# A fused cross-attention and maxout-FFN kernel: batch 0 loaded as fp32 by the hardware queue, batch 2 transposed by the array, token loads issued once per period

## The chip, the core and the metric

The kernel runs on one core of a Trainium2 chip. The core has a matrix array (TensorE, PE in the profile), three engines for element-wise work (VectorE or DVE, ScalarE or ACT, GpSimd or POOL) and a sequencer that issues DMAs and does no arithmetic (SyncE or SP). Each engine works through its own list of instructions in order, and engines wait for each other and for DMAs by semaphores. The array writes to a small memory of eight banks (PSUM), from which ACT or DVE copies results ("evicts" them) to the working memory. DMAs issued by SP and ACT go through a hardware queue, those issued by POOL through a software queue[...]. The metric is the device time of one execution, in microseconds.

## What is computed

There are 8 batches with 8 heads of 512 tokens and 32 state vectors, 64 wide. Tokens read the state, the state reads the tokens, and the 544 rows per batch go through a feed-forward layer with a maximum over three products:

```
scores  = x @ state.T / 8          # 512 x 32 per batch and head
xread   = softmax(scores)  @ state # 512 x 64
sread   = softmax(scores.T) @ x    # 32 x 64
r       = concat([xread, sread]), heads side by side   # 4352 x 512
h       = max(r @ w1, r @ w2, r @ w3)                  # 4352 x 768
out     = h @ w_out                                    # 4352 x 512, fp32
```

## The kernel before, in words

The state is first multiplied into the weights: for every batch b and every 128 columns m of the hidden layer, `m_unit` (M in the lists) forms M = state x W for all heads and three weight matrices. Each M unit is eight small matmuls into two banks, evicted by two copies of 384 columns on the engines that two letters name (aa: both on ACT, av: ACT and DVE). Then the hidden layer of the token rows is softmax x M. That is `up` (u): two matmuls into one bank for each of the three matrices i. For i = 0 ACT copies the bank (line 292), for i = 1 and 2 DVE takes the maximum with it (lines 296 and 298). `out_half` (o) multiplies the hidden rows with w_out, three matmuls for each half; after the second half a copy to fp32 and, after every two row tiles, a store of 512 KB on SP's queue (line 327).

The softmax of a batch needs these steps:

- `load_x` (lx, line 146): POOL issues a DMA that reads 1 MB of fp32 tokens and writes 512 KB of bf16. All batches lie side by side in one buffer, x_sb.
- `permute_x` (pm, line 207): a copy that brings the heads of a token together (tile xn), by the engine that the letter names (v DVE, g POOL, a ACT), for half of the token tiles or for all (a dash).
- the transposed tokens xT, in one of two ways: `x_array` (xT), eight transposing matmuls per half and a copy from the bank; or `x_crossbar` (xb, line 212), one transposing DMA on SP's queue.
- `scores` (S, two halves): 8 matmuls, exp on ACT (line 230), row sums and reciprocals on DVE (234, 237), and a multiply on POOL or DVE (238) into the tile a.
- the transposed softmax aT, by the array (`a_array`, aT) or by a transposing DMA (`a_crossbar`, ab or X, line 243).
- `state_reads` (R): the other direction, 24 matmuls, a reciprocal and two multiplies on DVE.

Nothing is ordered by a planner: every engine gets its instructions in the order in which the program emits them. That order is written by hand in three lists. OPENING (line 28) holds the first two batches' hidden layers and batch 0's output, token by token; `lw 0 1` loads W for columns of m = 0, `lo` loads w_out, `id`, `sel` and `idle` make the identity, transpose the state and run dummy matmuls. After it PERIOD runs six times and LAST once (loop from line 379). In a period, u belongs to the group g = 2, 3, 4, 5, 6 and then the state rows (group 8), o to the group before, S, X and R to the batch after (nb = t + 2), M to batches taken from a queue, and P permutes batch nb + 1 on POOL and transposes it by the crossbar. In LAST g is batch 7. The order of the letters is the order on the array; on POOL and SP the same order holds only among the few instructions that these engines get.

On POOL the order in the opening is: tokens 0, W (m = 0), tokens 1, W (4 and 5), permutations, W (1), W (2 and 3), tokens 2 and 3, two softmax multiplies, w_out, the permutation of batch 2, tokens 7, the permutation of batch 3, tokens 6 and 4, the multiplies of batch 2, tokens 5. From there on POOL only multiplies and permutes. SP issues the state load, the crossbar transposes of batches 2 and 3, and then for each period the transposes of a and of the next xn and two stores.

Of the kernel before, what the change touches and what calls it, by code (L numbers as in the profile page):

```python
# [8 lines left out]
F32 = mybir.dt.float32  # L9
BF16 = mybir.dt.bfloat16  # L10
# [15 lines left out]


OPENING = """
id, idle 9, sel, idle 9, lx 0, lw 0 1, lx 1, pm 0 0 v, lw 4 6, pm 0 1 g, lw 1 2,
xT 0 0 v, xT 0 1 v, pm 1 0 g, pm 1 1 g, S 0 0 v, M 2 0 aa, S 0 1 v, M 1 0 aa, idle 4,  # L30
lw 2 4, lx 2, M 0 0 aa, aT 0 0 v, R 0, xT 1 0 a, lx 3, aT 0 1 a, xT 1 1 v, S 1 0 g,
u 0 0 0, M 0 4 aa, M 0 5 av, u 0 0 1, u 0 0 2, S 1 1 g, lo, u 0 4 0, u 0 5 0, M 0 1 aa,
u 0 5 1, u 0 4 1, u 0 5 2, M 1 1 aa, u 0 4 2, M 1 4 aa, u 0 1 0, pm 2 - g, aT 1 - v,
xb 2, u 0 1 1, M 0 3 va, M 0 2 va, u 0 1 2, u 1 0 0, u 1 4 0, lx 7, pm 3 - g, u 1 1 0,
lx 6, u 1 0 1, u 0 3 0, u 1 4 1, u 0 2 0, M 1 2 aa, M 1 5 av, xb 3, u 1 4 2, u 0 2 1,
u 1 0 2, u 0 2 2, M 1 3 aa, M 2 3 aa, u 0 3 1, u 0 3 2, u 1 1 1, u 1 2 0, u 1 3 0,
u 1 5 0, u 1 1 2, u 1 5 1, lx 4, u 1 5 2, o 0 0 0 a, o 0 0 1 a, u 1 2 1, S 2 1 g,
S 2 0 g, ab 2, u 1 3 1, o 0 1 0 v, M 2 2 aa, R 1, o 0 1 1 a, o 0 2 0 v, M 2 4 aa,
u 1 2 2, o 0 2 1 a, o 0 3 0 a, M 2 5 aa, M 2 1 va, u 1 3 2, o 0 3 1 v, R 2, lx 5
"""  # L40


PERIOD = """
o o u u u u S S o o M M m u R u o u o X u u u u u u u P u u o u o u m M M
"""
LAST = """
M M u u u M u u S M u u u u u S u u u u P M R M u o u o u u o X o o o o o
"""


# [1 line left out]
def kernel(  # L52
# [14 lines left out]
    nc = tc.nc  # L67

    B, H, S, D = x.shape
# [5 lines left out]
    J = S // 128  # L75
# [6 lines left out]

    const = ctx.enter_context(tc.tile_pool(name="const", bufs=1))
    res = ctx.enter_context(tc.tile_pool(name="res", bufs=1))
    xnp = ctx.enter_context(tc.tile_pool(name="xnp", bufs=3))
    att2 = ctx.enter_context(tc.tile_pool(name="att2", bufs=2))
    tmpp = ctx.enter_context(tc.tile_pool(name="tmpp", bufs=4))
    htp = ctx.enter_context(tc.tile_pool(name="htp", bufs=2))
    op = ctx.enter_context(tc.tile_pool(name="op", bufs=2))
# [3 lines left out]
    def bank(shape, dt, name):  # L93
        return psum.tile(shape, dt, tag="bank", name=name)
# [3 lines left out]
    def copy(eng, o, i):  # L98
        if eng == "a":
            nc.scalar.copy(out=o, in_=i)  # L100
        else:
            ENG[eng].tensor_copy(out=o, in_=i)  # L102

    def mm(out_ap, lhsT, rhs, start, stop, pos=(0, 0)):
        nc.tensor.matmul(out_ap, lhsT, rhs, start=start, stop=stop, tile_position=pos)  # L105

    def tr(out_ap, in_ap):
# [8 lines left out]
    nc.sync.dma_start(  # L116
        out=st32.rearrange("p n d -> p (n d)"),
        in_=state.rearrange("b h (q n) d -> (b h q) (n d)", q=2))
    zeros = const.tile([128, 512], BF16, name="zeros")
    nc.vector.memset(zeros, 0.0)  # L120
    sbd = res.tile([128, B, HP, 2, Ns], BF16, name="sbd")
# [7 lines left out]

    W = res.tile([128, 3, HP, d_ff], BF16, name="W")  # L130
    wout = res.tile([128, MT, d_model], BF16, name="wout")
    x_sb = res.tile([128, B, H, J, D], BF16, name="x_sb")
    M_sb = res.tile([128, B, MT, 2, 3, 128], BF16, name="M_sb")
    AT = res.tile([128, HP, ST], BF16, name="AT")
    w_v = [w.rearrange("(kk p) f -> p kk f", p=128) for w in (moe_w1, moe_w2, moe_w3)]
# [6 lines left out]
    def load_wout():  # L142
        nc.gpsimd.dma_start(out=wout, in_=moe_w_out.rearrange("(kk p) f -> p kk f", p=128))

    def load_x(b):
        nc.gpsimd.dma_start(  # L146
            out=x_sb[:, b].rearrange("p h j d -> p h (j d)"),
            in_=x[b].rearrange("h (p j) d -> p h (j d)", j=J))


# [36 lines left out]
    def tile_of(kind, b, pool, shape):  # L187
        if (kind, b) not in tiles:
            tiles[kind, b] = pool.tile(shape, BF16, tag=kind, name=kind)
        return tiles[kind, b]  # L190

    def x_nat(b):
        return tile_of("xn", b, xnp, [128, J, H, D])

    def xT(b):
        return tile_of("xT", b, att2, [128, J, HP, 128])
# [9 lines left out]

    def permute_x(b, h, eng):
        j = slice(0, J) if h is None else slice(2 * h, 2 * h + 2)
        copy(eng, x_nat(b)[:, j], x_sb[:, b, :, j].rearrange("p h j d -> p j h d"))

    def x_crossbar(b):
        nc.sync.dma_start_transpose(
            out=xT(b).rearrange("p j hp t -> p (j hp) t"),
            in_=x_nat(b).rearrange("p j h d -> p (j h d)"))
# [27 lines left out]
    def a_crossbar(b):  # L242
        nc.sync.dma_start_transpose(
            out=aT(b).rearrange("p j a t -> p (j a) t"),
            in_=a_of(b).rearrange("p j a hp n -> p (j a hp n)"))
# [32 lines left out]
    def up(g, m, i):  # L278

        nn = S if g < B else ST  # L280
        ht = tile_of("ht", g, htp, [128, MT, S])
        pw = bank([128, S], F32, "pw")
        if g < B:
            for par in range(2):
                mm(pw, M_sb[:, g, m, par, i, :], aT(g)[:, :, par, :], par == 0, par == 1)
        else:
            for hp in range(HP):
                mm(pw[:, :nn], W[:, i, hp, m * 128:(m + 1) * 128], AT[:, hp, :],
                   hp == 0, hp == HP - 1)
        if i == 0:  # L290
            t = tiles["t", g, m] = tmpp.tile([128, S], BF16, tag="t0", name="t0")
            nc.scalar.copy(out=t[:, :nn], in_=pw[:, :nn])  # L292
        elif i == 1:
            t0 = tiles["t", g, m]
            t = tiles["t", g, m] = tmpp.tile([128, S], BF16, tag="t1", name="t1")
            nc.vector.tensor_max(t[:, :nn], t0[:, :nn], pw[:, :nn])  # L296
        else:
            nc.vector.tensor_max(ht[:, m, :nn], tiles["t", g, m][:, :nn], pw[:, :nn])  # L298

    def out_half(g, j, h, eng):  # L300
        last = g == ORDER[-1]
        if h == 0:
            tiles["po"] = bank([128, d_model], F32, "po")
        po = tiles["po"]
        for kt in range(3 * h, 3 * h + 3):
            mm(po, tiles["ht", g][:, kt, j * 128:(j + 1) * 128], wout[:, kt, :],
               kt == 0, kt == MT - 1)
        if h == 0:
            return
        rows = out[g * SP:g * SP + S, :].rearrange("(p j) f -> j p f", j=J) if g < B else None  # L310
        if last and j == J - 1:
            half = d_model // 2
            for k in range(2):
                o = op.tile([128, half], F32, tag=f"oh{k}", name=f"oh{k}")
                f = slice(k * half, k * half + half)
                copy("av"[k], o, po[:, f])
                (nc.scalar, nc.sync)[k].dma_start(out=rows[j][:, f], in_=o)
            return
        if j % 2 == 0:
            tiles["o"] = op.tile([128, 2, d_model], F32, tag="o", name="o")  # L320
        o = tiles["o"]
        copy(eng, o[:, j % 2, :], po)
        if last:
            nc.sync.dma_start(out=rows[j], in_=o[:, j % 2, :])
        elif g < B:
            if j % 2 == 1:
                nc.sync.dma_start(out=rows[j - 1:j + 1].rearrange("j p f -> p j f"), in_=o)
        else:
            for q in range(4):
                bb = 4 * j + q  # L330
                nc.sync.dma_start(out=out[bb * SP + S:(bb + 1) * SP, :],
                                  in_=o[q * 32:(q + 1) * 32, j % 2, :])
# [46 lines left out]
    for t in range(1, B):  # L379
        p, g = ORDER[t], ORDER[t + 1]  # L380
        nb = t + 2
        us = [(g, m, i) for m in range(MT) for i in range(3)]
        os = [(p, j, h) for j in range(J if p < B else ST // 128) for h in range(2)]
        sc = [0, 1]
        for what in (PERIOD if g != ORDER[-1] else LAST).split():
            if what == "u":
                up(*us.pop(0))
            elif what == "o":
                if os:
                    out_half(*os.pop(0), "a")  # L390
            elif what in ("M", "m"):
                if m_q:
                    m_unit(*m_q.pop(0), "aa" if what == "M" else "av")
            elif nb >= B:
                continue
            elif what == "S":
                scores(nb, sc.pop(0), "g")
            elif what == "P":
                if nb + 1 < B:
                    permute_x(nb + 1, None, "g")  # L400
                    x_crossbar(nb + 1)
            elif what == "R":
                state_reads(nb)
            elif what == "X":
                a_crossbar(nb)
    for j in range(J):
        for h in range(2):
            out_half(ORDER[-1], j, h, "a")
# [29 lines left out]
```

The softmax here doesn't subtract the row's maximum and nothing guards it: scores larger than these inputs give would overflow.

## Time and profile before

| | |
|---|---|
| six runs, us | 168.53 to 173.44, median 169.79 |
| profiled execution, us | 169.3, of which 167.5 from the first to the last instruction |
| mean granted clock of the array | 0.978 |
| busy: PE, DVE, ACT, POOL | 90%, 65%, 55%, 28% of the span |
| array's matmuls: u (two shapes), o | 80.1 us, 50.8 us |
| memory read, written | 15.20 MB, 8.91 MB |

The kernel's stages follow each other along the span: the opening up to about 54.6 us, six periods up to about 148, LAST with the last batch's output up to 163.8, and the last store. Busy shares over the whole span mix these stages, so they are read stage by stage. A line of the timeline has the start and length in us, the engine, the line of the program, the operation, the tiles it writes and reads, and how often; a bracket holds the time for which the engine stood idle before it and what ended that. A line with SPq or POOL and DMA is the time in which that engine issued the transfer, not the transfer itself.

### The profile page before, as it was taken

How to read it: one execution, taken by the hardware profiler on the slowest of the kernel's cores; microseconds unless marked ns; L12 is line 12 of the kernel's file. 1: busy time of each engine (PE TensorE's matmuls, PEld its weight loads, DVE VectorE, ACT ScalarE, POOL GpSimd, SP SyncE). 2: the span in 40 equal slices, each digit the busy share in tenths (PEclk: the TensorE clock that was granted, in tenths of full speed). 3: DMA queues.
4: the chain of work that ended last, by engine and by line, in shares of the span. 5: the costliest groups of instructions: out<-in, count | busy, mean ns of one | idle time of the engine just before them, and what ended most of it. 6: DMA issues, size and time to landing. Idle time of an engine off the chain costs nothing.

```text
span 167.5 us, 3476 instructions
## 1 busy us (share of the span) xinstructions
PE 150.9 (90%) x1353; PEld 74.2 (44%) x1370; DVE 109.4 (65%) x194; ACT 92.8 (55%) x190; POOL 46.7 (28%) x50
## 2 busy tenths in 40 slices
PE   7958899990499889999999999999999999999990
PEld 2445443340244344445445444454454466854440
DVE  3349998982175469949984986599479842659601
ACT  3527888741236095389458656874785383344440
POOL 8876963910060008005400710090022000000000
PEclk9999999998589999999999999999999999999999
DMA  4999999999999905533623391177306033030163
GB/s 129 145 180 197 179 194 195 194 125 135 159 178 158 286 29 165 130 125 122 146 48 125 129 188 74 51 162 159 127 4 188 0 125 129 0 125 0 46 201 131
DMA packets 37536, 21.71 MB, mean 130 GB/s; under 512 B 22672, under 2 KB 34960, under 8 KB 37520
## 3 DMA queue, kind: packets, MB, share of 16 engines
q0 software_dynamic: 15440, 7.34, 35.3%
q1 hardware_dynamic: 21936, 14.03, 32.9%
q8 instruction: 10, 0.16, 0.4%
q10 hardware_dynamic: 144, 0.13, 0.2%
q14 instruction: 6, 0.05, 0.2%
HBM read 15.20 MB, written 8.91 MB: 144 GB/s over the span
## 4 chain that ended last, share of the span: by engine, by line
PE 64%; DMA 25%; POOL 6%; issue 1%; DVE 1%; ACT 1%; ACTq 0%; POOLq 0%; DVEq 0%
PE pw L105 33%; PE po L105 23%; DMA x_sb<-in_x_dram 11%; DMA xT<-xn 9%; DMA out_dram<-o 5%; PE pm L105 4%; PE pr L105 3%; POOL xn L102 3%; POOL W L140 3%; PE ps L105 2%; POOL x_sb L146 1%; DVE ht L298 0%; DVE t L296 0%; ACT t L292 0%; DVE oh L102 0%
## 5 line engine op out<-in xcount | busy, mean ns | idle before, releaser
L105 PE MATMUL pw<-aT,M_sb 128*128 128x512 bf16 x288 | 71.3, 381 | 0.7 <-DMA aT<-a 0.6
L105 PE MATMUL po<-wout,ht 128*128 128x512 bf16 x189 | 50.8, 383 | 0.8 <-issue 0.2
L296 DVE TENSOR_TENSOR t<-t,pw 128x512 bf16<-128x512 bf16 (+1 forms) x54 | 35.2, 653 | 23.2 <-ACT t L292 14.8
L292 ACT CAST t<-pw 128x512 bf16<-128x512 f32 (+1 forms) x54 | 30.1, 570 | 27.8 <-PE pw L105 26.1
L105 PEld LDWEIGHTS <-M_sb 128*128 128x128 bf16 x288 | 26.4, 98 | 33.3 <-issue 3.7
L298 DVE TENSOR_TENSOR ht<-t,pw 128x512 bf16<-128x512 bf16 (+1 forms) x54 | 35.3, 657 | 6.9 <-PE pw L105 3.2
L100 ACT CAST M_sb<-pm 128x384 bf16<-128x384 f32 x81 | 33.2, 504 | 5.6 <-PE pm L105 5.6
L238 POOL TENSOR_TENSOR a<-e,rden 128x512 bf16<-128x512 bf16 x14 | 14.4, 1045 | 73.1 <-ACT e L230 46.8
L100 ACT COPY o<-po 128x512 f32<-128x512 f32 x32 | 19.1, 596 | 21.0 <-PE po L105 15.6
L105 PEld LDWEIGHTS <-ht 128*128 128x128 bf16 x204 | 19.2, 99 | 22.4 <-issue 2.4
L102 POOL COPY xn<-x_sb 128x2048 bf16<-128x2048 bf16 (+1 forms) x9 | 15.1, 1686 | 6.2 <-DMA x_sb<-in_x_dram 6.2
L230 ACT ACTIVATE e<-ps 128x512 bf16<-128x512 f32 x16 | 9.0, 605 | 11.6 <-PE ps L105 11.5
L234 DVE TENSOR_REDUCE den<-e 128x16 f32<-128x512 bf16 x16 | 10.6, 663 | 7.3 <-ACT e L230 7.1
L105 PE MATMUL pm<-W,sbd 64*32 64x384 bf16 x384 | 12.6, 328 | 1.2 <-DMA W<-in_moe_w_dram 0.7
L105 PE MATMUL ps<-sbd,xT 128*128 128x64 bf16 x128 | 5.8, 199 | 6.4 <-DMA xT<-xn 6.3
L105 PEld LDWEIGHTS <-sbd 64*32 64x32 bf16 x384 | 4.3, 89 | 11.4 <-issue 11.1
L140 POOL DMA_DIRECT2D W<-in_moe_w_dram x12 | 9.0, 767 | 0.0
L105 PEld LDWEIGHTS <-xT 128*128 128x128 bf16 x128 | 5.2, 102 | 8.6 <-DMA xT<-xn 6.8
L105 PE MATMUL pw<-AT,W 128*128 128x256 bf16 x72 | 8.8, 273 | 0.0
L102 DVE CAST M_sb<-pm 128x384 bf16<-128x384 f32 x15 | 7.9, 533 | 1.4 <-PE pm L105 1.3
L271 DVE RECIPROCAL rd<-pr 128x128 f32<-128x128 f32 x8 | 7.6, 950 | 0.8 <-PE pr L105 0.6
L105 PE MATMUL pz<-zeros 128*128 128x512 bf16 x20 | 6.9, 495 | 1.2 <-DVE zeros L120 1.2
(38 smaller groups left out, 65.2 us busy)
## 6 DMA issues: line engine op xcount, KB each, us to landing
out_dram<-o SPq DMA_DIRECT2D x14, 512.0 KB, 2.7
x_sb<-in_x_dram POOLq DMA_DIRECT2D x8, 512.0 KB, 10.0
W<-in_moe_w_dram POOLq DMA_DIRECT2D x6, 256.0 KB, 8.4
W<-in_moe_w_dram POOLq DMA_DIRECT2D x6, 128.0 KB, 8.2
wout<-in_moe_w_out_dram POOLq DMA_DIRECT2D x1, 768.0 KB, 10.8
out_dram<-o SPq DMA_DIRECT2D x3, 256.0 KB, 2.1
st<-in_state_dram SPq DMA_DIRECT2D x1, 512.0 KB, 3.5
out_dram<-o SPq DMA_DIRECT2D x8, 64.0 KB, 1.7
```

What stands on the lines that cost most here:

```text
L100: nc.scalar.copy(out=o, in_=i)
L102: ENG[eng].tensor_copy(out=o, in_=i)
L105: nc.tensor.matmul(out_ap, lhsT, rhs, start=start, stop=stop, tile_position=pos)
L140: nc.gpsimd.dma_start(out=W[:, i, :, c], in_=w_v[i][:, :, c])
L146: nc.gpsimd.dma_start(out=x_sb[:, b].rearrange("p h j d -> p h (j d)"), in_=x[b].rearrange("h (p j) d -> p h (j d)", j=J))
L230: nc.scalar.activation(out=e.rearrange("p r n -> p (r n)"), in_=ps.rearrange("p j a hp n -> p (j a hp n)"), func=AF.Exp, scale=scale)
L234: nc.vector.reduce_sum(out=den, in_=e, axis=AX.X)
L238: ENG[eng].tensor_mul(out=a_of(b)[:, 2 * h:2 * h + 2].rearrange("p j a hp n -> p (j a hp) n"), in0=e, in1=rden.unsqueeze(2).to_broadcast(( ...
L271: nc.vector.reciprocal(out=rd, in_=pd.rearrange("p (hp n) -> p hp n", hp=HP))
L292: nc.scalar.copy(out=t[:, :nn], in_=pw[:, :nn])
L296: nc.vector.tensor_max(t[:, :nn], t0[:, :nn], pw[:, :nn])
L298: nc.vector.tensor_max(ht[:, m, :nn], tiles["t", g, m][:, :nn], pw[:, :nn])
```

## The change

- Batch 0's tokens are loaded as fp32 into a buffer of their own (x32, 1 MB) by SP's hardware queue, right behind the state. `permute_x` of batch 0 reads that buffer and converts; its halves go to ACT and DVE.
- The batches 1 to 7 get buffers from a pool of four (xlp) in place of one buffer for all.
- OPENING is a new list. Batch 1's tokens are the first load on POOL, ahead of W, whose parts come as m = 0, then 2 and 3, then 1, then 4 and 5; tokens 2 and 3 and w_out follow, and no more tokens. Batch 1's permutation goes to DVE. The transposed halves of batch 2 are made by the array; batch 3's stay with the crossbar. The softmax multiplies of batch 0 go from DVE to POOL, and there are 25 dummy matmuls for 22. Units of the hidden layer come in another order.
- PERIOD and LAST are new orders of the same units, and have a new letter L, which loads the tokens of batch nb + 1 on POOL, after the first three u's of a period. A period begins with u where it began with output halves, and the two groups of three M units have their second eviction on DVE twice each (m M m) where it was once (M M m).
- The two half tiles of the very last output get buffers of their own.

```
--- before.py
+++ after.py
@@ -26,25 +26,25 @@
 
 
 OPENING = """
-id, idle 9, sel, idle 9, lx 0, lw 0 1, lx 1, pm 0 0 v, lw 4 6, pm 0 1 g, lw 1 2,
-xT 0 0 v, xT 0 1 v, pm 1 0 g, pm 1 1 g, S 0 0 v, M 2 0 aa, S 0 1 v, M 1 0 aa, idle 4,
-lw 2 4, lx 2, M 0 0 aa, aT 0 0 v, R 0, xT 1 0 a, lx 3, aT 0 1 a, xT 1 1 v, S 1 0 g,
-u 0 0 0, M 0 4 aa, M 0 5 av, u 0 0 1, u 0 0 2, S 1 1 g, lo, u 0 4 0, u 0 5 0, M 0 1 aa,
-u 0 5 1, u 0 4 1, u 0 5 2, M 1 1 aa, u 0 4 2, M 1 4 aa, u 0 1 0, pm 2 - g, aT 1 - v,
-xb 2, u 0 1 1, M 0 3 va, M 0 2 va, u 0 1 2, u 1 0 0, u 1 4 0, lx 7, pm 3 - g, u 1 1 0,
-lx 6, u 1 0 1, u 0 3 0, u 1 4 1, u 0 2 0, M 1 2 aa, M 1 5 av, xb 3, u 1 4 2, u 0 2 1,
-u 1 0 2, u 0 2 2, M 1 3 aa, M 2 3 aa, u 0 3 1, u 0 3 2, u 1 1 1, u 1 2 0, u 1 3 0,
-u 1 5 0, u 1 1 2, u 1 5 1, lx 4, u 1 5 2, o 0 0 0 a, o 0 0 1 a, u 1 2 1, S 2 1 g,
-S 2 0 g, ab 2, u 1 3 1, o 0 1 0 v, M 2 2 aa, R 1, o 0 1 1 a, o 0 2 0 v, M 2 4 aa,
-u 1 2 2, o 0 2 1 a, o 0 3 0 a, M 2 5 aa, M 2 1 va, u 1 3 2, o 0 3 1 v, R 2, lx 5
+id, idle 9, sel, idle 9, pm 0 0 a, lx 1, pm 0 1 v, pm 1 0 v, lw 0 1, xT 0 0 a, lw 2 4,
+pm 1 1 v, xT 0 1 a, lw 1 2, S 0 0 g, S 0 1 g, xT 1 0 a, xT 1 1 v, M 0 0 aa, M 1 0 av,
+R 0, lw 4 6, S 1 1 g, lx 2, S 1 0 g, aT 0 0 a, idle 7, aT 0 1 a, M 0 3 aa, M 0 2 aa,
+M 1 2 va, R 1, u 0 0 0, u 0 3 0, M 0 1 va, u 0 0 1, u 0 3 1, u 0 2 0, aT 1 - v, M 1 3 aa,
+u 0 1 0, u 0 3 2, u 0 0 2, lx 3, u 0 1 1, M 0 5 aa, M 0 4 va, u 1 2 0, u 0 2 1, lo,
+pm 2 - g, u 1 0 0, u 1 2 1, pm 3 - g, M 2 5 av, M 1 5 av, u 0 1 2, u 0 5 0, xb 3,
+u 0 4 0, u 0 2 2, u 1 3 0, xT 2 0 a, u 0 5 1, u 0 5 2, M 1 4 aa, M 1 1 aa, u 0 4 1,
+xT 2 1 v, u 1 2 2, u 1 0 1, u 0 4 2, S 2 0 g, u 1 3 1, u 1 1 0, u 1 5 0, S 2 1 g,
+u 1 4 0, o 0 0 0 v, o 0 0 1 a, o 0 1 0 a, u 1 0 2, o 0 1 1 a, u 1 5 1, M 2 2 aa, ab 2,
+M 2 3 aa, M 2 0 av, o 0 2 0 a, u 1 4 1, o 0 2 1 a, u 1 3 2, M 2 4 aa, M 2 1 aa, u 1 5 2,
+u 1 1 1, R 2, o 0 3 0 v, o 0 3 1 a, u 1 1 2, u 1 4 2
 """
 
 
 PERIOD = """
-o o u u u u S S o o M M m u R u o u o X u u u u u u u P u u o u o u m M M
+u u u L u u S u S X o o u u P o o m M m u R u o o u m M m u u u u u u o u o
 """
 LAST = """
-M M u u u M u u S M u u u u u S u u u u P M R M u o u o u u o X o o o o o
+u u M M u u P u u u L S u R o S u u M X u u o M u u u M u u o M u o o o o o
 """
 
 
@@ -82,6 +82,7 @@
 
     const = ctx.enter_context(tc.tile_pool(name="const", bufs=1))
     res = ctx.enter_context(tc.tile_pool(name="res", bufs=1))
+    xlp = ctx.enter_context(tc.tile_pool(name="xlp", bufs=4))
     xnp = ctx.enter_context(tc.tile_pool(name="xnp", bufs=3))
     att2 = ctx.enter_context(tc.tile_pool(name="att2", bufs=2))
     tmpp = ctx.enter_context(tc.tile_pool(name="tmpp", bufs=4))
@@ -116,6 +117,10 @@
     nc.sync.dma_start(
         out=st32.rearrange("p n d -> p (n d)"),
         in_=state.rearrange("b h (q n) d -> (b h q) (n d)", q=2))
+
+    x32 = res.tile([128, H, J, D], F32, name="x32")
+    nc.sync.dma_start(out=x32.rearrange("p h j d -> p h (j d)"),
+                      in_=x[0].rearrange("h (p j) d -> p h (j d)", j=J))
     zeros = const.tile([128, 512], BF16, name="zeros")
     nc.vector.memset(zeros, 0.0)
     sbd = res.tile([128, B, HP, 2, Ns], BF16, name="sbd")
@@ -129,7 +134,6 @@
 
     W = res.tile([128, 3, HP, d_ff], BF16, name="W")
     wout = res.tile([128, MT, d_model], BF16, name="wout")
-    x_sb = res.tile([128, B, H, J, D], BF16, name="x_sb")
     M_sb = res.tile([128, B, MT, 2, 3, 128], BF16, name="M_sb")
     AT = res.tile([128, HP, ST], BF16, name="AT")
     w_v = [w.rearrange("(kk p) f -> p kk f", p=128) for w in (moe_w1, moe_w2, moe_w3)]
@@ -142,9 +146,12 @@
     def load_wout():
         nc.gpsimd.dma_start(out=wout, in_=moe_w_out.rearrange("(kk p) f -> p kk f", p=128))
 
+    x_sb = {}
+
     def load_x(b):
+        x_sb[b] = xlp.tile([128, H, J, D], BF16, tag="x", name="x")
         nc.gpsimd.dma_start(
-            out=x_sb[:, b].rearrange("p h j d -> p h (j d)"),
+            out=x_sb[b].rearrange("p h j d -> p h (j d)"),
             in_=x[b].rearrange("h (p j) d -> p h (j d)", j=J))
 
 
@@ -206,7 +213,8 @@
 
     def permute_x(b, h, eng):
         j = slice(0, J) if h is None else slice(2 * h, 2 * h + 2)
-        copy(eng, x_nat(b)[:, j], x_sb[:, b, :, j].rearrange("p h j d -> p j h d"))
+        i = x_sb[b][:, :, j] if b else x32[:, :, j]
+        copy(eng, x_nat(b)[:, j], i.rearrange("p h j d -> p j h d"))
 
     def x_crossbar(b):
         nc.sync.dma_start_transpose(
@@ -311,7 +319,7 @@
         if last and j == J - 1:
             half = d_model // 2
             for k in range(2):
-                o = op.tile([128, half], F32, tag=f"oh{k}", name=f"oh{k}")
+                o = res.tile([128, half], F32, name=f"oh{k}")
                 f = slice(k * half, k * half + half)
                 copy("av"[k], o, po[:, f])
                 (nc.scalar, nc.sync)[k].dma_start(out=rows[j][:, f], in_=o)
@@ -399,6 +407,9 @@
                 if nb + 1 < B:
                     permute_x(nb + 1, None, "g")
                     x_crossbar(nb + 1)
+            elif what == "L":
+                if nb + 1 < B:
+                    load_x(nb + 1)
             elif what == "R":
                 state_reads(nb)
             elif what == "X":
```

More of the change, by code (lines that the diff above doesn't have):

```diff
@@ L28 @@
 OPENING = """
[L29 to L39, printed above, removed]
+id, idle 9, sel, idle 9, pm 0 0 a, lx 1, pm 0 1 v, pm 1 0 v, lw 0 1, xT 0 0 a, lw 2 4,
+pm 1 1 v, xT 0 1 a, lw 1 2, S 0 0 g, S 0 1 g, xT 1 0 a, xT 1 1 v, M 0 0 aa, M 1 0 av,
+R 0, lw 4 6, S 1 1 g, lx 2, S 1 0 g, aT 0 0 a, idle 7, aT 0 1 a, M 0 3 aa, M 0 2 aa,
+M 1 2 va, R 1, u 0 0 0, u 0 3 0, M 0 1 va, u 0 0 1, u 0 3 1, u 0 2 0, aT 1 - v, M 1 3 aa,
+u 0 1 0, u 0 3 2, u 0 0 2, lx 3, u 0 1 1, M 0 5 aa, M 0 4 va, u 1 2 0, u 0 2 1, lo,
+pm 2 - g, u 1 0 0, u 1 2 1, pm 3 - g, M 2 5 av, M 1 5 av, u 0 1 2, u 0 5 0, xb 3,
+u 0 4 0, u 0 2 2, u 1 3 0, xT 2 0 a, u 0 5 1, u 0 5 2, M 1 4 aa, M 1 1 aa, u 0 4 1,
+xT 2 1 v, u 1 2 2, u 1 0 1, u 0 4 2, S 2 0 g, u 1 3 1, u 1 1 0, u 1 5 0, S 2 1 g,
+u 1 4 0, o 0 0 0 v, o 0 0 1 a, o 0 1 0 a, u 1 0 2, o 0 1 1 a, u 1 5 1, M 2 2 aa, ab 2,
+M 2 3 aa, M 2 0 av, o 0 2 0 a, u 1 4 1, o 0 2 1 a, u 1 3 2, M 2 4 aa, M 2 1 aa, u 1 5 2,
+u 1 1 1, R 2, o 0 3 0 v, o 0 3 1 a, u 1 1 2, u 1 4 2
 """
 PERIOD = """
-o o u u u u S S o o M M m u R u o u o X u u u u u u u P u u o u o u m M M
+u u u L u u S u S X o o u u P o o m M m u R u o o u m M m u u u u u u o u o
 """
 LAST = """
-M M u u u M u u S M u u u u u S u u u u P M R M u o u o u u o X o o o o o
+u u M M u u P u u u L S u R o S u u M X u u o M u u u M u u o M u o o o o o
 """
@@ L84 @@
     res = ctx.enter_context(tc.tile_pool(name="res", bufs=1))
+    xlp = ctx.enter_context(tc.tile_pool(name="xlp", bufs=4))
     xnp = ctx.enter_context(tc.tile_pool(name="xnp", bufs=3))
@@ L118 @@
         in_=state.rearrange("b h (q n) d -> (b h q) (n d)", q=2))
+    x32 = res.tile([128, H, J, D], F32, name="x32")
+    nc.sync.dma_start(out=x32.rearrange("p h j d -> p h (j d)"),
+                      in_=x[0].rearrange("h (p j) d -> p h (j d)", j=J))
     zeros = const.tile([128, 512], BF16, name="zeros")
@@ L131 @@
     wout = res.tile([128, MT, d_model], BF16, name="wout")
-    x_sb = res.tile([128, B, H, J, D], BF16, name="x_sb")
     M_sb = res.tile([128, B, MT, 2, 3, 128], BF16, name="M_sb")
@@ L143, in load_wout @@
         nc.gpsimd.dma_start(out=wout, in_=moe_w_out.rearrange("(kk p) f -> p kk f", p=128))
+    x_sb = {}
     def load_x(b):
+        x_sb[b] = xlp.tile([128, H, J, D], BF16, tag="x", name="x")
         nc.gpsimd.dma_start(
-            out=x_sb[:, b].rearrange("p h j d -> p h (j d)"),
+            out=x_sb[b].rearrange("p h j d -> p h (j d)"),
             in_=x[b].rearrange("h (p j) d -> p h (j d)", j=J))
@@ L208, in permute_x @@
         j = slice(0, J) if h is None else slice(2 * h, 2 * h + 2)
-        copy(eng, x_nat(b)[:, j], x_sb[:, b, :, j].rearrange("p h j d -> p j h d"))
+        i = x_sb[b][:, :, j] if b else x32[:, :, j]
+        copy(eng, x_nat(b)[:, j], i.rearrange("p h j d -> p j h d"))
     def x_crossbar(b):
@@ L313, in out_half @@
             for k in range(2):
-                o = op.tile([128, half], F32, tag=f"oh{k}", name=f"oh{k}")
+                o = res.tile([128, half], F32, name=f"oh{k}")
                 f = slice(k * half, k * half + half)
@@ L401 @@
                     x_crossbar(nb + 1)
+            elif what == "L":
+                if nb + 1 < B:
+                    load_x(nb + 1)
             elif what == "R":
```

## The prediction

> **What bounds the kernel now.** I read the stages first, then the waits of the array, then the DMA queues. The stage view gives busy time of the five engines, granted clock, DMA share (over 1 when packets overlap on a DMA engine) and GB/s.
>
> ```profile
> 9.80:17.50 7.70, 6.67 (x115) 4.57 (x117) 6.41 (x12) 4.87 (x10) 6.31 (x8) 1.00 1.48 191
> 17.50:38.10 20.60, 19.82 (x179) 7.98 (x176) 18.08 (x31) 15.18 (x33) 12.36 (x12) 1.00 1.43 178
> 38.10:44.37 6.27, 0.00 (x0) 0.00 (x1) 0.69 (x1) 0.18 (x1) 0.00 (x0) 0.70 1.51 135
> 44.37:54.62 10.25, 10.09 (x119) 5.04 (x120) 6.35 (x12) 5.22 (x11) 2.93 (x3) 0.85 1.30 170
> 54.62:71.93 17.31, 16.15 (x151) 7.47 (x149) 12.64 (x23) 8.66 (x18) 3.87 (x3) 1.00 0.51 146
> 71.93:87.70 15.77, 15.66 (x155) 7.46 (x149) 12.05 (x22) 10.58 (x23) 3.88 (x3) 1.00 0.40 117
> ```
>
> From 71.93 on a period takes 15.77 us with the array busy 15.66: there the array is the bound and nothing is to be had. All slack lies before: one hole of 6.27 us, a slow clock behind it, and a first period of 17.31 where the others need 15.77. The waits name the hole, and the queue lines the reason:
>
> ```profile
> PE ps L105 <- DMA xT<-xn: 6.3, 1, 6.3
> ```
>
> ```profile
> 29.62 14.65 SPq L212 DMA_TRANSPOSE xT<-xn  x2
> 66.32 1.60 SPq L212 DMA_TRANSPOSE xT<-xn  x1
> ```
>
> ```profile
> 29.54 0.87 POOL L146 DMA_DIRECT2D x_sb<-in_x_dram  x1
> 32.25 1.75 POOL L146 DMA_DIRECT2D x_sb<-in_x_dram  x2
> 48.83 0.94 POOL L146 DMA_DIRECT2D x_sb<-in_x_dram  x1
> ```
>
> The scores of batch 2 wait from 38.1 to 44.3 for a crossbar transpose begun at 29.62. It ran beside three token loads and took 14.7 us; the tile view of xT gives 3.6/3.8/17.2 us to landing (least, median, most), so 3.8 is the price without loads.
>
> **Part by part.** Costs of units on the array, from its back-to-back stretches in the chain: u 0.43 us, output half 0.65, M 0.20, half of scores 0.24, state reads 0.81; a transposed half of xT 0.44 (8 weight loads in 0.45 us). The old opening sums to 35.6 us of array time, the new one to 37.2: two more transposed halves (0.9) and three more dummy matmuls (0.65). Every period sums to 15.4 in both lists.
>
> *Batch 0 as fp32 by SP's queue.* Before, its load is issued at 1.43 on POOL and its permutation starts at 9.3. Now SP issues it at about 1.15 behind the state load (512 KB, landed in 3.5 us), and the same 1 MB is read from memory. The Trainium skill speaks against a gain: "DMA: Bandwidth & Descriptors", section Issuing engines are not separate DMA queues, has all queues interleave on the same 16 engines, so another queue saves only issue time. With that page's price for one DMA (2.0 us and bytes over 436 GB/s, section Anatomy of one DMA) the estimate is 1.15 + 1.2 + 2.4 + 2.0 = 6.8 us alone; sharing with batch 1's 1 MB, at most 2.4 more, 9.2. The row: stage 9.8 to 17.5 moves 191 GB/s as written, 382 as read, so 2.5 MB of state and tokens need 6.5 us from about 1.5, plus a landing, near 9. No fp32 load of this shape is in the trace. I take 8.5, bounds 6.8 to 10.
>
> The permutation moves from POOL/DVE (1.29 and 0.43 us, bf16) to ACT for half 0: the state's fp32 cast of 1024 elements took 1.04. DVE's fp32 half is not in the trace; between 0.43 (bf16) and 1.3 (POOL's copy), I take 1.0. Both start at 8.5. Then ACT evicts both transposed halves (1.01 each, where DVE took 0.69). So: permuted 9.6, first half evicted 11.1, second 12.1, scores 1 done 12.4 (before: 12.5). No gain; each microsecond of landing shifts it equally.
>
> *Between that and the first u.* Batch 1 lies second in the list now (its permutation on DVE, 2 x 0.43, stands in front of batch 0's softmax; landed near 9 to 11 it is in time). On the array come R 0, both scores of 1, a transposed half, seven dummies, R 1. They wait on ACT and DVE: two exps by 13.3, R 0 to 14.2, the xT halves of batch 1 evicted by 15.3, its scores to 15.8, dummies and aT to 17.8, three M and R 1 to 19.2. The old order reaches its first u at 17.5, but has 26.5 us of list left where the new one has 25.95.
>
> *The rest of the opening.* From 17.5 to 38.1 the old one put 18.4 us of list into 20.6, 89%, with DVE at 88%. At 89%, 25.95 takes 29 us: end near 48. Two checks. DVE from the first scores: 24 maxima x 0.685, 6 softmax halves x 0.92, 3 state reads x 1.53, 7 M halves x 0.53, 3 copies x 0.69, together 32.3 us; from 12.6 at 88 to 94% it ends at 47 to 49.3. ACT: 31 us from 12.1, lighter. POOL and loads: x2, x3 and wout stand in the queue behind the same bytes as before (st, two tokens, all of W). Before, POOL waited for batch 2 until 27.7, so permutation ends near 29.6; the new list needs it at xT 2 (9.4 us of list after the first u, so near 29.7). Just in time; one or two microseconds of wait are possible. Batch 2 by the array costs 0.9 us of array, one 1.01 copy on ACT and one 0.69 on DVE, counted above. Batch 3's crossbar starts near 32.3 beside wout alone (landed 34.3 before) and isn't due until 50.
>
> So the hole (6.3), the half clock behind it (about 1.5 us: 16 score matmuls 0.85 where 0.47 is usual) and other waits go: old opening end 54.62, new 48, gain 6.6. The old first period lost 17.31 - 15.77 = 1.5 to a store of 8.45 us beside the load at 48.83; its output copy now falls before that. Gain 1.5.
>
> *Loads moved into periods.* L stands after three u's, but that orders POOL's list, not its time. It needs no array result, its buffer (four of them, seven batches) is long free, so POOL issues it as soon as the previous period's permutation is done. That is the moment at which SP starts that batch's crossbar (before: permutation 64.42 to 66.30, crossbar 66.32). **Load and crossbar are not apart:** loads 5, 6, 7 start about 1 us behind crossbars 4, 5, 6. Load 4 follows the softmax of batch 2, near 41, beside batch 0's store and the transpose of a for batch 2.
>
> Price, from the page's list of queues (packets, MB, share of 16 engines):
>
> ```profile
> q0 software_dynamic: 15440, 7.34, 35.3%
> ```
>
> That is 61 ns a packet; a token load has 8 heads x 128 rows = 1024 of 512 B, so 3.9 us. A transpose of xT, 3.8 less about 2 of landing, moves in 1.8. Together 5.7 to 6.8 (the stretch 29.5 to 58.6 took some 15% more than such a sum) and 2: 7.7 to 8.8 after issue. A skill rule says it costs nothing: "DMA: Bandwidth & Descriptors", Rules for kernel authors, has a transpose next to ordinary DMAs need nothing (a rule of safety, yet readable as free), and "Advanced Engine Details and Errata", X-Bar Transpose, calls it as fast as regular DMAs, hence 3.8. The 14.7 row disagrees; I take the row's side at one load instead of three.
>
> Due date: scores at 2.2 of the next period; issue at S 3.1 + exp, den, two POOL multiplies of 1.03 (6.5) + permutation 1.9 = 8.4. So 15.8 + 2.2 - 8.4 = 9.6 us for 7.7 to 8.8: covered by about one. The store behind it on SP waits for its issue and lands near 18; its buffer is wanted at 20. The transpose of a is issued first and has 9 us for 3.1. For batch 2 it is worse: store, then a's transpose at 42.5 beside load 4; 1.3 + 0.9 + 3.9 + 2 gives up to 50.4, wanted at 48 since the period now begins with u. Like row: 48.90 to 56.7 with one load, 7.8 us. I charge 1.5 (0 to 3).
>
> *Period order, M split, pools.* Two more M halves per period go to DVE (12.05 + 1.1 of 15.77); ACT falls to 9.5. Covered by the array. LAST has the same units; oh in another pool changes no wait of weight. Bounds for the new orders: -0.3 (15.44 is the list sum) to +0.5 per period; taken 0.
>
> **Sum.** 169.3 (profiled, span 167.5 and 1.8 around it) - 6.6 - 1.5 + 1.5 = 162.7. The profiled execution lies 0.5 under the median of 169.79; I leave that and say 162.6.
>
> **Rivals.**
> A, crossbars late (13%, the slower side): each of the three takes 14.7 as at 29.62 instead of under 8.8. For: that row; the array's order leaves one microsecond. Against: there it met three loads and wout. It passes the due date by 5.1, three times 15.3, and a hole over 3 us brought 0.70 clock above, some 1.5 each: 162.6 + 15.3 + 4.5 = 182. Decision point: past 12.0 us of landing the three stalls (2.4 each) eat the gain.
> B, crossbars a little late (20%): 10.5 to 11.5 us, 1 to 2 each, and up to 3 for a's transpose: 165 to 168.5.
> C, the opening is bound elsewhere (12%): tokens land at 10, loads or DVE hold the list to 80% instead of 89: 25.95 / 0.8 = 32.4, ends 51.6: 166.
> D, fp32 lands at 7 and loads are free (part of the main case): 159.5.
>
> **Numbers.** Main case 55%: 162.6, own range 159.5 to 165. B 20, C 12, A 13. Holding eight in ten: 159.5 to 168. Faster by over 1% (a measurement here separates about 1%): 0.79; within 1%: 0.08 (the upper edge of B and C, a weak A); slower: 0.13.
>
> **What would show it.** Right: no wait over 2 us of the scores of batch 2; opening done (state reads of batch 2) near 46 to 49; crossbars of xT landing in 7 to 9 us while a token load runs, each load issued where POOL's permutation ends; periods of 15.8; clock 1.00 from 12 us on. Wrong: a hole ahead of the scores in periods two to four (A, B); POOL or DVE waiting for tokens beyond 11 us (C); loads issued well away from crossbars; a first u before 17 or after 21.

## The result and the profile after

| | before | after |
|---|---|---|
| median of all runs, us | 169.32 (63 runs, 167.66 to 173.44) | 169.36 (28 runs, 166.06 to 174.03) |
| ratio after to before | | 0.989, 95% interval 0.986 to 0.992 |
| profiled execution, us (span) | 169.3 (167.5) | 169.26 (167.2) |

The ratio compares only the executions within 1.5% of each kernel's fastest, 51 of the 63 before and 8 of the 28 after, so it lies under that of the medians. The new kernel's time varies more from run to run than the old one's, from 166.06 to 174.03 us with granted clocks from 1.00 down to 0.96; the profiled execution lies in the middle of that. Forecast was 162.6, with 159.5 to 168.0 as range: the time is at best 1.4% down, where 4% was forecast.

The stage view of the changed kernel has the same columns as before (five engines, clock, DMA share, GB/s):

```profile
19.00:45.30 26.30, 26.19 (x261) 12.11 (x262) 22.19 (x38) 19.49 (x42) 10.00 (x9) 1.00 1.02 153
44.00:49.40 5.40, 2.29 (x12) 0.91 (x12) 2.91 (x6) 0.59 (x1) 0.00 (x0) 1.00 1.35 174
66.00:69.20 3.20, 1.54 (x10) 0.57 (x9) 1.97 (x3) 1.01 (x2) 0.00 (x0) 1.00 1.31 286
84.90:87.50 2.60, 0.21 (x3) 0.05 (x3) 1.23 (x2) 0.36 (x1) 0.00 (x0) 1.00 1.24 307
87.50:92.00 4.50, 4.50 (x28) 1.91 (x29) 2.33 (x5) 1.80 (x4) 1.76 (x2) 0.62 0.27 105
```

The opening has become dense: from 19.0 on the array hardly rests, and the hole of 6.3 us at 38.1 is gone. In its place are three smaller holes, at 46, 67 and 85 us, all with the DMA engines busy, and after the third a stretch at a clock of 0.62. The array's timeline says what each hole waits for (the bracket at the end of a line):

```profile
49.37 2.33 PE L106 MATMUL pw<-aT,M_sb 128*128 128x512 bf16 x10 [3.06 <-DMA aT<-a]
51.54 0.40 PE L106 MATMUL ps<-sbd,xT 128*128 128x64 bf16 x8
69.13 0.41 PE L106 MATMUL ps<-sbd,xT 128*128 128x64 bf16 x8 [1.66 <-DMA xT<-xn]
87.46 0.41 PE L106 MATMUL ps<-sbd,xT 128*128 128x64 bf16 x8 [2.39 <-DMA xT<-xn]
104.92 0.40 PE L106 MATMUL ps<-sbd,xT 128*128 128x64 bf16 x8
120.69 0.40 PE L106 MATMUL ps<-sbd,xT 128*128 128x64 bf16 x8
```

Each hole ends with a transposing DMA. The distances of the first scores of each period price them: 17.59, 18.33, 17.46 and 15.77. The last period has no load beside its crossbar; against it the others lose 1.82, 2.56 and 1.69 (the third one to the slow clock, in which six output matmuls take 2.75 us for 1.46, and not to a wait). That is 6.1 us, and 3.1 at the first hole.

The issue lines of the two queues show the meeting; POOL's come first, then SP's, in two views of the same kernel:

```profile
56.32 1.89 POOL L103 COPY xn<-x 128x2048 bf16<-128x2048 bf16 x1
58.16 0.94 POOL L153 DMA_DIRECT2D x<-in_x_dram  x1
75.75 0.94 POOL L153 DMA_DIRECT2D x<-in_x_dram  x1
94.09 0.94 POOL L153 DMA_DIRECT2D x<-in_x_dram  x1
```

```profile
58.24 2.20 SPq L220 DMA_TRANSPOSE xT<-xn  x1
75.84 2.60 SPq L220 DMA_TRANSPOSE xT<-xn  x1
94.17 3.26 SPq L220 DMA_TRANSPOSE xT<-xn  x1
112.20 1.60 SPq L220 DMA_TRANSPOSE xT<-xn  x1
```

Load and crossbar are issued 0.08 to 0.09 us apart, three times. By the tile view of xT the four crossbars landed 10.8, 11.6, 10.3 and, without a load, 3.6 us after issue; the loads beside them took 11.5, 13.1 and 11.6. The view over all five crossbars (least, median, most):

```profile
DMA to landing us min/median/max: 3.6/10.3/11.6
```

The third made the array wait for nothing: the slow clock just before had put off its scores, which came 10.75 us after its issue, where the two others were wanted after 9.2 (for the first, 69.13 less the wait of 1.66, less 58.24). The transpose of a at 39.61, beside the load issued at 38.70, took 9.7 where the others took 3.0 to 4.9.

### The profile page after: what moved, and what is told of

Read it like the earlier page. It is cut to its first block, busy times and chain, and to the rows that moved or that the text cites. A ratio compares the mean times of both kernels' runs of the same rounds, so it can differ in the third digit from the quotient of the medians.

```text
span 167.2 us, 3519 instructions
## 1 busy us (share of the span) xinstructions
PE 151.3 (90%) x1371; PEld 75.2 (45%) x1389; DVE 112.2 (67%) x203; ACT 93.7 (56%) x184; POOL 44.6 (27%) x48
## 4 chain that ended last, share of the span: by engine, by line
PE 45%; DMA 7%; issue 0%; DVE 0%; ACT 0%
PE pw L106 23%; PE po L106 17%; DMA xT<-xn 7%; PE pm L106 2%; PE pr L106 1%; PE ps L106 1%; DVE oh L103 0%; ACT oh L101 0%
## 5 line engine op out<-in xcount | busy, mean ns | idle before, releaser
L106 PE MATMUL pw<-aT,M_sb 128*128 128x512 bf16 x288 | 72.6, 382 | 3.3 <-DMA aT<-a 3.1
L106 PE MATMUL po<-wout,ht 128*128 128x512 bf16 x188 | 50.0, 387 | 0.6
L106 PEld LDWEIGHTS <-M_sb 128*128 128x128 bf16 x288 | 25.9, 98 | 36.0 <-issue 5.9
L246 POOL TENSOR_TENSOR a<-e,rden 128x512 bf16<-128x512 bf16 x16 | 16.6, 1040 | 72.5 <-ACT e L238 48.7
L101 ACT CAST M_sb<-pm 128x384 bf16<-128x384 f32 x69 | 28.4, 497 | 2.2 <-PE pm L106 1.5
L103 DVE CAST M_sb<-pm 128x384 bf16<-128x384 f32 x27 | 14.0, 551 | 3.4 <-PE pm L106 3.3
L103 POOL COPY xn<-x 128x2048 bf16<-128x2048 bf16 x6 | 11.3, 1892 | 4.9 <-DMA x<-in_x_dram 4.9
L106 PE MATMUL pm<-W,sbd 64*32 64x384 bf16 x384 | 11.5, 326 | 0.4 <-DMA W<-in_moe_w_dram 0.4
L106 PE MATMUL pz<-zeros 128*128 128x512 bf16 x23 | 7.6, 479 | 1.2 <-DVE zeros L125 1.2
L106 PEld LDWEIGHTS <-W 128*128 128x128 bf16 x72 | 7.0, 98 | 1.9
```

Source lines behind the costliest of these rows:

```text
L246: ENG[eng].tensor_mul(out=a_of(b)[:, 2 * h:2 * h + 2].rearrange("p j a hp n -> p (j a hp) n"), in0=e, in1=rden.unsqueeze(2).to_broadcast(( ...
```

## The experiments

Theory 1: a token load in flight keeps a crossbar transpose for several microseconds more than its own size, and nothing else is wrong with the changed kernel. Theory 2: the stores do it, or only all three together. Theory 3: the new order of the periods has stalls of its own. All times are medians of four executions, ratios are to the kernel before on the same chip.

### Without the loads

```
 def load_x(b):
+    if b > 3:
+        x_sb[b] = x_sb[3]
+        return
```

> Left out: the loads of the tokens of batches 4 to 7 (the permutations read batch 3's tokens again, so those batches' output rows are not theirs). Everything else stands. Theory 1 (a token load in flight keeps the crossbar): all transposes of xT land in 3.6 to 4.5 us and those of a in 3 to 4, the scores never wait for a DMA, the clock stays at 1.00 after the start, and the time is that of the changed kernel less its four stalls and slow clock (3.1 + 1.8 + 2.6 + 1.7 = 9.2): about 160, ratio to the kernel before near 0.945. Theory 2 (it is the store, or the three together): xT lands at 6 us or later, time 162 or more. Theory 3 (the new order of the periods has too early a due time or stalls of its own): stalls remain at the start of periods, time 164 or more.

160.50 us, ratio 0.949 (0.944 to 0.955). No wait of the scores or of u for a DMA is left, the clock is 0.997, and the four executions lie within 0.9 us. Crossbars land in 3.7 to 5.3 us (those of batches 4 to 6 in 5.3, 4.6 and 4.6):

```profile
DMA to landing us min/median/max: 3.7/4.6/5.3
```

That is 8.9 us less than the changed kernel, where 9.2 were expected. The loads' presence is the whole loss. It doesn't say yet that it is their moment.

### The same loads, held back

```
-u u u L u u S u S X ... u m M m u u u u u u o u o
+u u u u u S u S X ... u m M m u u u L u u u o u o
-lo,
+lo, lx 4,
...
             elif what == "L":
-                if nb + 1 < B:
-                    load_x(nb + 1)
+                if nb + 2 < B:
+                    nc.gpsimd.tensor_copy(out=gate, in_=tiles["ht", g][:, 3, 0:1])
+                    load_x(nb + 2)
```

> All loads stay, at another time: batch 4's right behind w_out in the opening, batches 5 to 7 one period ahead, each behind a copy of one element on GpSimd that reads the hidden rows of column block 3, so that it is issued at about 12.5 to 13 us of the period, when the crossbar of that period has landed. Theory 1: as without loads, 159.5 to 161, the transposes of xT at 3.6 to 4.5; the second store of a period takes the collision instead and lands in 6 to 8 us, for which nothing waits. Theory 2: 164 or more, since stores still meet loads. Theory 3: 164 or more.

160.70 us, ratio 0.948 (0.940 to 0.956), with all of the work done. POOL's lines in this kernel:

```profile
60.73 0.94 POOL L154 DMA_DIRECT2D x<-in_x_dram  x1
76.78 0.94 POOL L154 DMA_DIRECT2D x<-in_x_dram  x1 [0.26 <-issue]
92.91 0.94 POOL L154 DMA_DIRECT2D x<-in_x_dram  x1 [0.26 <-DVE t L305]
```

Its crossbars are issued at 56.07, 71.85 and 87.65, so each load now starts about 5 us behind. These crossbars land in 5.6, 4.7 and 4.3 us, the loads in 7.5, 5.7 and 6.3. Batch 3's crossbar in the opening meets the load of batch 4 now and takes 7.3 us, for which nothing waits. The same bytes at another time cost nothing: theory 1, and the moment is the cause.

### Without the stores beside the crossbar

```
-                nc.sync.dma_start(out=rows[j - 1:j + 1]...
+                if j == 3 or g not in (1, 2, 3):
+                    nc.sync.dma_start(out=rows[j - 1:j + 1]...
```

> Left out: the first store (row tiles 0 and 1) of batches 1, 2 and 3, the one that SP issues right behind the crossbar beside the load. Theory 1: transposes of xT of batches 4 to 6 still land after 9.5 us or more, stalls of 1 us or more remain, time within 1.5 us of the changed kernel's. Theory 2: they land in under 7 us and the time falls by 4 or more, to 165 or less.

171.38 us, ratio 1.014 (1.006 to 1.023). The crossbars of batches 4 to 6 land in 9.2, 11.8 and 10.2 us: theory 2 falls, the store has no visible share. The time is 2 us over the changed kernel's median, more than was expected. In its profile the array ran at a clock of 0.56 from 50 to 56 us, behind the hole of 3.1, and at 0.72 from 90 to 95, behind one of 2.6; the changed kernel's profile has one such stretch. Its times (170.3 to 172.7) lie within the changed kernel's, but why all four have slow stretches wasn't settled.

### The old order of the periods

With the loads at the front of PERIOD, and with the loads held back:

```
-u u u L u u S u S X o o u u P o o m M m ...
+L o o u u u u S S o o M M m u R u o u o X u u u u u u u P u u ...
```
```
+o o u u u u S S o o M M m u R u o u o X u u u u u u u P L u u ...
```

> The new opening with the old order of PERIOD and LAST, the load put at the front of PERIOD, so that it is issued as in the changed kernel. Theory 1: the load still starts with the crossbar, xT lands after 10 us or more, and since the order moves issue and due date together the scores still wait about 2 us in each of the periods two to four; the transpose of a has 1.3 us more before it is wanted, so its stall falls to about 2: 166 to 169.5. Theory 3 (the new order of the periods costs the time): 160 to 163.

> The new opening and the held-back loads with the old order of PERIOD and LAST, the load behind P and held back by the same one-element copy. If the order of the periods is neutral once no load meets a crossbar: within 0.7 us of the kernel with held-back loads in the new order, 160 to 161.4. If the old order is better by itself (the run with the old order and the load at its front took 165.75 where the changed kernel took 169.36): 158.5 or less.

With the loads beside the crossbars: 165.75 us (161.73 to 167.47), just under the 166 to 169.5 that theory 1 expected; the four lie too far apart for a ratio. The profiled execution is the fastest of them: a's transpose makes the array wait 1.4 us, and the crossbars land in 8.8, 9.0 and 8.7, just inside the 9.3 us that they have (73.47 to 82.75 for the second). Theory 1 expected 10 or more there; with the load issued at the same moment, the length still differs from order to order and, to judge by the spread of the times, perhaps from run to run. What shortens it here stays open (a store issued 6 us later is no explanation, by the run without stores). Held back, the order doesn't matter: 161.21, ratio 0.952 (0.946 to 0.958) against 0.948 (0.940 to 0.956). Theory 3 falls.

### The kernel before, without its loads of batches 4 to 7

```
 def load_x(b):
+    if b > 3:
+        return
...
-    copy(eng, x_nat(b)[:, j], x_sb[:, b, :, j]...
+    copy(eng, x_nat(b)[:, j], x_sb[:, min(b, 3), :, j]...
```

> The kernel before, whole, without its loads of the tokens of batches 4 to 7 (left out; the permutations read batch 3's tokens again). Theory 1: the hole ahead of the scores of batch 2 comes from these loads, so it closes: the crossbar of batch 2 lands within 8 us of 29.6, next to what is left of w_out, the second one in 4 to 5 after; with the hole (6.3), the slow clock behind it (1.5) and the first period's 1.5 gone the time is near 160 to 161.5. Rival (the hole comes from the long list of W and w_out in front, or from the crossbar's late start): 164 or more.

160.19 us, ratio 0.948 (0.940 to 0.956). The hole is gone and the first crossbar lands in 6.6 us instead of 14.7. That is no more than the changed kernel takes without the same loads (160.50). So all that the changed kernel could win over the kernel before was this one collision, and of its other parts none is worth anything that this shows.

### The parts of the change, undone one at a time

Both start from the kernel with held-back loads. First, batch 0 by the software queue again; second, batch 2 by the crossbar again.

```
-    x32 = res.tile([128, H, J, D], F32, name="x32")
-    nc.sync.dma_start(out=x32..., in_=x[0]...)
-id, idle 9, sel, idle 9, pm 0 0 a,
+id, idle 9, sel, idle 9, lx 0, pm 0 0 a,
```
```
-... xT 2 0 a, ... xT 2 1 v, ...
+pm 2 - g, xb 2, u 1 0 0, ...
```

> The kernel with held-back loads (160.7 measured), with one part of the change undone: batch 0's tokens come as bf16 by GpSimd's software queue, first in its list, in a buffer of the pool; the permutations stay on ScalarE and VectorE. Theory H (the hardware queue is worth its place): batch 0 lands near 9.3 us as in the kernel before, where it landed at 7.6; batch 1 and all of W come later by the load's share in the queue, 2 to 4 us, and the opening ends 2 to 4 us later: 162.5 to 165. Rival (one set of DMA engines, only issue time saved): the same bytes are read, 160.5 to 161.7.

> The kernel with held-back loads, with the other part undone: batch 2 is transposed by the crossbar right after its permutation, while the loads of batch 3, of w_out and of batch 4 are under way. Theory 1: this crossbar lands after 10 us or more, where its scores follow 5 us after the permutation, so that the array stands 4 us or more: 164 to 168, with a slow clock in some runs. Rival (the array's transposes cost as much as they save): 159.8, 0.9 us of array time less than the kernel with held-back loads.

Software queue: 161.85 us, ratio 0.954 (0.946 to 0.962), between the two expectations. Batch 0 lands at 10.0 us instead of 8.3 and batch 1 at 13.0 instead of 10.6. The array waits 3.1 us for its first tokens instead of 1.2, and the time is 1.2 us longer; but the intervals overlap, so a gain from this part isn't shown, and by the two ratios it is three microseconds at most. Crossbar for batch 2: 169.31, ratio 0.987 (0.981 to 0.994). Its landing took 10.1 us beside the loads of batch 3, of w_out and of batch 4:

```profile
38.30 0.61 PE L107 MATMUL ps<-sbd,xT 128*128 128x64 bf16 x8 [5.69 <-DMA xT<-xn]
```

A hole of 5.69 us, and a clock of 0.58 from 36 to 44, around its end. By the medians that costs 8.6 us, by the ratios 6.7. So the array's transposes, at 0.9 us of array time, keep the opening dense once all three loads stand there. Without batch 4's load they need not: in the kernel before without its late loads, batch 2's crossbar met w_out alone, landed in 6.6 us, and there was no hole.

### Half of each load

```
-            out=x_sb[b].rearrange(...), in_=x[b].rearrange(...)
+            out=x_sb[b][:, 0:nh].rearrange(...), in_=x[b, 0:nh].rearrange(...)   # nh = H if b < 4 else H // 2
```

> The changed kernel with half of each load of batches 4 to 7 at the same moment (heads 0 to 3 alone; left out are heads 4 to 7 of these batches, and the permutations read batch 3's tokens again, so the rows of batches 4 to 7 are not theirs). Alone a whole load lands in 5.9 us and a crossbar in 3.6 to 4.3; both together took 10.3 to 11.6. If they add up and no more, the crossbar beside half a load lands in 5.6 to 6.0. If the transfers slow each other for as long as both run, the excess scales with the load: 7 to 8.2. In either case it is under the 9.6 us that are free, so no waits of the scores: 160.5 to 162, with the transpose of a of batch 2 at 6 to 7 us and no wait or one under 1 us.

160.22 us, ratio 0.947 (0.941 to 0.952). Crossbars in 7.6, 7.3 and 6.4 us; two of the three lie in the 7 to 8.2 expected of transfers that slow each other, the third below. Over the same crossbars without loads (5.3, 4.6 and 4.6) that is 2.3, 2.7 and 1.8, where a whole load brings 5.5, 7.0 and 5.7: twice the load brings more than twice the excess. The prediction's estimate for the movement of a whole load is 3.9 us, so some 2 for a half. A sum of sizes fits the half load, and falls short of what the whole one does by 1.6 to 3.1 us.

### One queue or two

The same loads in the same part of the period as fp32, first on SP's queue right behind the crossbar, then on ScalarE's queue beside it.

```
+    def load_x32(b, q=None):
+        x_sb[b] = xfp.tile([128, H, J, D], F32, tag="xf", name="xf")   # one buffer
+        (q or nc.sync).dma_start(out=x_sb[b]..., in_=x[b]...)
...
                     x_crossbar(nb + 1)
+                if nb + 2 < B:
+                    load_x32(nb + 2)            # SP's queue
...
             elif what == "L":                   # or: L behind m M m, and
+                if nb + 2 < B:
+                    load_x32(nb + 2, nc.scalar)
```

> The changed kernel with the tokens of batches 4 to 7 loaded as fp32 by SP's own queue, each put right behind the crossbar it met before (the first behind the transpose of a of batch 2), into one fp32 buffer; GpSimd's permutation converts. Same moment, same bytes read, twice the bytes written, one queue for both. Theory Q (it is the two queues' packets in turn that slow each other; one queue works its transfers off in order): the transposes of xT land in 3.6 to 5 us, the load behind in 6 to 7.5, no waits, 160 to 161.5. Rival M (any load in flight slows a crossbar, whatever its queue): xT in 7 us or later, with waits of the scores where it passes 9.6, 163 or more.

> As the run with the loads on SP's queue, but the fp32 loads of batches 5 to 7 are issued by ScalarE on its own hardware queue, in its list behind the copies of the first three M units, so that they start where the crossbar of the same period does (they wait for the permutation that frees the buffer). No change of type on the way and no software queue, yet a second queue. If two queues' packets in turn are what slows a crossbar (theory Q): xT lands in 7 to 11 us, 160.5 to 168 depending on whether it passes the 9.6 that are free. If only the software queue's loads do it (theory S): xT in 3.6 to 5 us and 159.5 to 161.

SP's queue: 159.91 us, ratio 0.947 (0.940 to 0.954), all work done, no wait of the array for a DMA of a period. SP's lines and the tile view of xT:

```profile
55.19 1.61 SPq L226 DMA_TRANSPOSE xT<-xn  x1
56.90 0.53 SPq L154 DMA_DIRECT2D xf<-in_x_dram  x1
```

```profile
DMA to landing us min/median/max: 3.6/4.9/5.3
```

The crossbars that have a load behind them land in 5.1, 4.6 and 4.9 us, as without loads, although the load is issued before they have landed, 1.7 to 3.0 us behind; the loads land 6.5 to 8.6 us after issue, in time. On ScalarE's queue the loads of batches 5 to 7 are issued beside the crossbar (batch 4's stays on SP's queue). ScalarE's lines, SP's, and the tile view of xT:

```profile
55.74 0.44 ACTq L154 DMA_DIRECT2D xf<-in_x_dram  x1
71.71 0.38 ACTq L154 DMA_DIRECT2D xf<-in_x_dram  x1
87.77 0.37 ACTq L154 DMA_DIRECT2D xf<-in_x_dram  x1
```

```profile
55.73 4.93 SPq L226 DMA_TRANSPOSE xT<-xn  x1
71.70 6.46 SPq L226 DMA_TRANSPOSE xT<-xn  x1
87.77 8.28 SPq L226 DMA_TRANSPOSE xT<-xn  x1
```

```profile
DMA to landing us min/median/max: 3.7/9.3/10.5
```

162.28 us, ratio 0.953 (0.948 to 0.958), with crossbars of 9.3, 9.4 and 10.5; the scores behind the last of them start 1.3 us late, at 98.36, as it lands. The intervals of the two runs overlap, so it is the landings that tell them apart. Neither the software queue nor the change of type is needed: a load issued at the same moment on either other queue delays the crossbar, and one behind it on its own queue doesn't.

Theory Q expected both, but its mechanism, packets of two queues in turn, isn't shown. The delay sits in different places: beside ScalarE's load SP spends 4.9 to 8.3 us on issuing the crossbar, which lands 2.2 to 4.4 us after that; beside GpSimd's, in the changed kernel, the issue takes 2.2 to 3.3 and the landing another 7.0 to 9.0. Nor were queue and moment changed apart: on SP's queue the crossbar had a start of 1.7 to 3.0 us, on ScalarE's 0.01 at most. On the software queue a start of 3.5 us was enough (held back in the old order: 4.5, 4.3 and 4.3); one of 2 us on another queue wasn't run.

## Why the prediction was wrong

The forecast had the mechanism and its place: L is not held where it stands in the list, load and crossbar meet, the transpose of a for batch 2 is worst off. It had the price wrong. Its sum against the profiled execution:

| term | forecast, us | measured, us |
|---|---|---|
| opening (hole, slow clock, waits), to the end of its list | -6.6 (end at 48) | -8.4 (46.2) |
| first period's stall at 54 to 72 | -1.5 | -1.5 |
| wait for a's transpose | +1.5 (0 to 3) | +3.1 |
| three crossbars (two of which the array waited for) | 0 ("covered by about one") | +4.4 |
| slow clock behind a hole | 0 | +1.7 |
| after the array's end | 0 | +0.7 |
| sum | -6.6 | 0.0 |

The opening's end follows from the array's timeline: the last two u's of its list, and with them the list, end at 46.2.

**The step that failed** is the price of a crossbar beside one load: "Together 5.7 to 6.8 ... 7.7 to 8.8 after issue". Each of the two on its own is near what the sum took: a load lands in 5.7 to 6.3 us where it meets little, a crossbar in 3.6 to 5.3 without loads. Adding them was wrong. Together they took 10.3 to 11.6, which is 1.5 to 3.9 us more than forecast. Why two transfers take longer than one after the other stays open. The 15% on top came from a stretch of the kernel before and didn't carry over. The row of one load beside a's transpose (7.8 us) was at hand too, and taken for a check; in the new kernel load and transpose took 9.7, with a store issued just before, so one row was no bound. (Two sums are off by 0.2, which decides nothing: 5.7 and 15% are 6.6, not 6.8, and the terms of a's transpose end at 50.6, not 50.4.)

**The slack was nearly right** (9.6 us forecast from issue to due, 9.2 by the lines), so a miss of about 2 us went into the time undiminished, twice. The third crossbar was as late, but the slow clock had put off its scores. Rival B described this, with 10.5 to 11.5 us and 165 to 168.5, and got a fifth of the chances. The quickest executions (from 166.06) lie in its range. Its end was too low for the others, since it left out that a hole can cost a slow clock behind it. That has no fixed price: the hole of 3.06 us at 46.3 left the clock at 1.00, the one of 2.39 at 85 took it to 0.62. It is the likely reason why the executions spread over 8 us, where those without holes lie within 0.9 (without loads) and 1.7 (held back); only one of the 28 has a trace.

**The opening** came out 1.8 us better: from the first u at 19.0 (forecast 19.2) the 25.95 us of list took 27.2, 95% and not 89. The 89% of the kernel before was no share of waiting: by the row shown with it, the array was busy for 19.82 of its 20.60 us. Whether VectorE, at 88% then and 84% in 19.0 to 45.3 now, set it isn't shown. Batch 0's fp32 tokens landed at 7.6 (8.5 assumed), ScalarE converted its half in 1.045 us, VectorE in 0.69 (1.0 assumed). None of it is shown to have gained anything, as the undone hardware load says.

**The rules of the Trainium skill.** That a transpose next to ordinary DMAs needs nothing ("DMA: Bandwidth & Descriptors", Rules for kernel authors), read as a price, and that it is as fast as a regular DMA ("Advanced Engine Details and Errata", X-Bar Transpose) would have made the three crossbars 3.8 us; without loads they are near that, with 3.6 to 5.3. Beside a load on another queue they are not, with 8.7 to 11.8, and setting the rules aside was right. The price for one DMA with which batch 0's load was estimated ("DMA: Bandwidth & Descriptors", Anatomy of one DMA) stands there for GpSimd's path, and that load went by SP's; it landed at 7.6, between the 6.8 and 9.2 that were worked out. That another queue saves only issue time (same page, Issuing engines are not separate DMA queues) can't be told from batch 0's time, 161.85 against 160.70, though its landing at 8.3 instead of 10.0 speaks for more. For a crossbar the choice of queue and place together made 4.6 to 5.1 or 9.3 to 10.5.

**Rival A** (14.7 us each, 182) asked for three loads at once and didn't come; C (a slow opening) was refuted by the dense array.

## What to carry to other kernels

A DMA issue in a hand-written order starts when its own engine gets to it, not where it stands among the others' work: look at what that engine waits for just before, and give it something to wait for, or put it behind the transfer that it must not meet, in the same queue. Don't price two transfers in flight as the sum of their sizes when one is a crossbar transpose; look for a row in which just these two meet. A slack of one microsecond on a step that recurs is no cover: its miss can be paid in each period, and a hole of two or three microseconds on the array may cost the clock as well.

## What the runs showed of the hardware

- A crossbar of 512 KB lands in 3.6 to 5.3 us without loads, in 9.3 to 10.5 beside a load of 1 MB issued at the same moment on ScalarE's hardware queue, in 9.2 to 11.8 (8.7 to 9.0 in the old order of the periods) beside one on GpSimd's software queue, and in 4.6 to 5.1 with that load 1.7 to 3.0 us behind it on SP's own queue.
- Beside ScalarE's loads the issue of the crossbar on SP took 4.9 to 8.3 us, beside GpSimd's, issued at the same moment, 1.9 to 3.3, in the kernel without loads 1.6 to 2.6.
- ScalarE's three loads hardly suffer from the crossbar: 6.4, 7.8 and 8.5 us, where SP's behind it took 6.5 to 8.6. The software queue's do: 11.5 to 13.1 (8.8 to 9.3 in the old order of the periods) instead of 5.7 to 7.5 when held back.
- GpSimd's permuting copy of 2048 elements takes 1.89 us from fp32 as from bf16.
- Behind holes of 2.4 to 3.1 us on the array the clock was 0.56 to 0.72 over the next four to six microseconds in three cases, and 1.00 in one.
